# Gated linear attention on one core: the steps in a new order and on other engines, and second inputs of GpSimd's additions two elements further

## The chip, the cores and the metric

The kernel runs on one core of a Trainium2 chip. The metric is the device time of one execution in microseconds (us). Five engines work side by side and meet through semaphores: TensorE (PE in the profile, its weight loads PEld), VectorE (DVE), ScalarE (ACT), GpSimd (POOL) and SyncE (SP), which issues all transfers here.

## The reference

Linear attention over 8 batches of 8 heads, followed by a gated projection with a causal convolution of five taps as the gate:

```python
q_s = exp(q - max(q, axis=-1)); q_s = q_s / (sum(q_s, axis=-1) + 1e-09)
k_s = exp(k - max(k, axis=2));  k_s = k_s / (sum(k_s, axis=2) + 1e-09)
kv = einsum('bhsd,bhse->bhde', k_s, v)
x = einsum('bhsd,bhde->bhse', q_s, kv)          # then (B, S, H * D) = (8, 576, 512)
gate_pre = sum over k of conv_w[k] * x shifted down by 4 - k rows
gate = 1 / (1 + exp(-gate_pre))
out = (gate * (x @ w_val)) @ w_out
```

All inputs are float32 (the weights arrive as 64-bit words, whose value the kernel rebuilds).

## The kernel before

One string, ORDER, names 975 steps. The kernel records them one by one, each on the engine that its last letter names (v VectorE, p GpSimd, a ScalarE), so each engine works through its own part of that string in order and waits where an operand isn't there. No loop and no scheduler decides anything.

First, eight slabs of weight words (steps load_words, part, field, scaled, signed, joined) become two float32 values each, a rounded high part and a rest (w_high, w_low). Beside that, for each batch b of eight: the softmax over q (q_max, q_sub, q_exp, q_sum; in batches 0 to 2 also q_mul and transposes by TensorE, in batches 3 to 7 a second copy of q with channels on partitions, from which the row values ql that q_spread has fetched are subtracted: qc_sub, qc_exp), the softmax over k (k_peak, k_row, k_spread fetch the maxima kmax; k_sub, k_exp), and then

- kv b and kv_norm: the product of k and v, one 64 by 64 block per head;
- attend b 0 and attend b 1: TensorE makes x, channels on partitions, 576 tokens, two blocks p of 128 channels each;
- for each block p: x_high and x_low split x in two parts; first b p and four steps tap b p j sum the convolution into the tile gate. A tap on VectorE is one instruction that reads x from PSUM and gate from SBUF. A tap that is written "a" is two: ScalarE makes the product far from x, then GpSimd adds far to gate, both in SBUF. Step sigmoid follows.

Tokens are then cut into nine runs i of 512 (8 x 576 = 9 x 512). value i m is 12 matmuls of 128x512 (three products of high and low parts over four blocks); gated i m j multiplies by the gate into the tile g; g_high and g_low split g; project i t is again 12 matmuls, and store i t scales by 0.5 and writes out. Run i needs x of batch i - 1 and, below 8, of batch i.

Line numbers in the profile: 283 and 288 k_sub, 367 q_sub, 380 q_mul, 432 qc_sub, 237 and 236 signed, 229 field, 515 a tap on VectorE, 518 and 519 its two instructions elsewhere, 501 x_low, 542 gated, 183 and 181 copies (x_high, g_high), 550 g_low, 535 value, 559 project, 479 attend, 450 kv.

Of the kernel before, what the change touches and what calls it, by code (L numbers as in the profile page):

```python
# [48 lines left out]
    k_raise 1 2, load_words 5, signed 1, kv_norm 0 0 a, kv_norm 0 1 a, q_sum 1 a, q_turn 0 0, q_turned 0 0 a, w_low 2
    p, q_mul 1 2 p, load_kc 1 1, k_top 1 1, q_turn 0 1, q_turn 0 3, q_mul 1 0 v, q_turned 0 1 a, attend 0 0,  # L50
    load_words 4, field 4, q_mul 1 3 p, w_high 3 a, q_turned 0 3 a, w_low 3 v, first 0 0 a, tap 0 0 1 v, q_mul 1 1 p,
    q_turn 1 1, first 0 1 a, tap 0 1 2 a, load_kc 1 0, k_top 1 0, load_km 2 1, scaled 4 a, signed 4, part 1 a, joined
# [579 lines left out]
```

## Time and profile before

| | us |
|---|---|
| median of 3 runs (lowest, highest) | 322.35 (321.4, 323.44) |
| the profiled execution | 324.02 |
| its span, first to last instruction | 322.2 |
| busy in the span: PE, DVE, POOL, ACT | 272.3, 271.6, 229.0, 201.8 |

The profile is one execution. Its span lacks 1.8 us of its own time, and that execution lies 1.7 us above the median of the runs. Busy time is not work: an instruction that has been started and waits for its operands' ports counts as busy, and a matmul's recorded length overlaps the next one's. How long a matmul holds the engine is read from a long chain of them, as length over count.

### The profile page before, as it was taken

The numbers are of one execution on the slowest core, as the hardware profiler recorded it, in microseconds if no ns is written. First come the engines' busy times: TensorE is split into PE (matmuls) and PEld (weight loads), VectorE is DVE, ScalarE is ACT, GpSimd is POOL, SyncE is SP. The second block draws the span as 40 slices with busy tenths as digits, with TensorE's granted clock in tenths as the row PEclk, the third lists the DMA queues.
The fourth block names the chain that finished last, engine by engine and source line by source line (L and its number), as shares of the span: only waits on it lengthen the run. The fifth ranks groups of instructions, "written<-read, shape, count | busy, mean of one in ns | idle before, by whom it ended". The sixth has DMA issues, their size and how long they took to land.

```text
span 322.2 us, 5134 instructions
## 1 busy us (share of the span) xinstructions
PE 272.3 (85%) x1854; PEld 206.8 (64%) x1854; DVE 271.6 (84%) x399; ACT 201.8 (63%) x318; POOL 229.0 (71%) x187
## 2 busy tenths in 40 slices
PE   0264526899988999989999899999899999999995
PEld 0154413677766578757877586777577867888883
DVE  3999999999999999998999998999967886672330
ACT  2694776888789559885968696488715546431011
POOL 2696879489997899989878788788734935165210
PEclk9998755999999999999999999999979999999999
DMA  7999167449887756984948769953746201000123
GB/s 237 386 389 399 35 240 316 163 179 379 303 294 241 221 121 215 355 262 103 269 168 215 190 235 291 257 170 157 228 174 167 73 2 65 33 35 1 65 79 117
DMA packets 21800, 63.05 MB, mean 196 GB/s; under 512 B 3472, under 2 KB 7696, under 8 KB 18448
## 3 DMA queue, kind: packets, MB, share of 16 engines
q1 hardware_dynamic: 21776, 62.74, 57.8%
q8 instruction: 14, 0.23, 0.3%
q14 instruction: 10, 0.08, 0.1%
HBM read 53.19 MB, written 9.54 MB: 195 GB/s over the span
## 4 chain that ended last, share of the span: by engine, by line
DVE 50%; PE 28%; DMA 6%; issue 6%; ACT 5%; POOL 3%; SPq 0%; DVEq 0%; ACTq 0%; POOLq 0%
PE out L559 17%; PE val L535 9%; DVE gate L515 8%; DVE qs L374 5%; DVE xx L501 4%; DVE qm L364 4%; DVE g L542 3%; DMA ql<-qrow 3%; DVE kpk L269 3%; DVE qT L432 3%; DVE k L283 2%; DVE e L237 2%; DVE e L229 2%; DVE e L236 2%; PE x L479 2%
## 5 line engine op out<-in xcount | busy, mean ns | idle before, releaser
L519 POOL TENSOR_TENSOR gate<-gate,far 128x573 f32<-128x573 f32 (+3 forms) x57 | 79.2, 1394 | 40.0 <-ACT far L518 38.7
L535 PE MATMUL val<-xx,w_val_hi 128*128 128x512 f32 x288 | 89.9, 393 | 0.9 <-DVE xx L501 0.9
L535 PEld LDWEIGHTS val<-xx,w_val_hi 128*128 128x128 f32 x288 | 54.1, 188 | 12.7 <-DVE xx L501 1.3
L535 PE MATMUL val<-xx,w_val_lo 128*128 128x512 f32 x144 | 58.2, 404 | 3.5 <-DVE g L542 1.2
L559 PE MATMUL out<-w_out_lo,gh 128*128 128x512 f32 x144 | 58.7, 407 | 2.3 <-DVE gh L183 1.8
L559 PE MATMUL out<-w_out_hi,gl 128*128 128x512 f32 x144 | 58.0, 403 | 2.6 <-DVE gl L550 2.4
L515 DVE SCALAR_TENSOR_TENSOR gate<-x,cw,gate 128x572 f32<-128x572 f32 (+3 forms) x71 | 56.5, 806 | 1.3 <-POOL gate L519 0.4
L559 PE MATMUL out<-w_out_hi,gh 128*128 128x512 f32 x144 | 57.4, 399 | 0.0
L518 ACT ACTIVATE far<-x,cw 128x573 f32<-128x573 f32 (+3 forms) x57 | 41.5, 747 | 22.7 <-DVE gate L515 11.1
L550 POOL TENSOR_TENSOR gl<-g,gh 128x512 fp32r<-128x512 f32 x24 | 31.9, 1336 | 13.8 <-PE out L559 6.4
L542 DVE SCALAR_TENSOR_TENSOR g<-gate,val 128x320 f32<-128x320 f32 (+7 forms) x64 | 26.8, 446 | 12.4 <-POOL gl L550 5.3
L367 POOL TENSOR_TENSOR q<-q,qm 128x576 f32<-128x576 f32 x24 | 31.9, 1347 | 6.2 <-DVE qm L364 3.1
L535 PEld LDWEIGHTS val<-xx,w_val_lo 128*128 128x128 f32 x144 | 27.0, 188 | 14.0 <-issue 3.9
L187 ACT ACTIVATE o<-out 128x512 f32<-128x512 f32 x27 | 16.0, 601 | 31.8 <-PE out L559 16.2
L559 PEld LDWEIGHTS out<-w_out_lo,gh 128*128 128x128 f32 x144 | 27.4, 190 | 11.8 <-DVE gh L183 3.5
L559 PEld LDWEIGHTS out<-w_out_hi,gl 128*128 128x128 f32 x144 | 27.4, 190 | 11.3 <-DVE gl L550 4.2
L559 PEld LDWEIGHTS out<-w_out_hi,gh 128*128 128x128 f32 x144 | 27.5, 191 | 6.2
L501 DVE TENSOR_TENSOR xx<-x,xx 128x512 fp32r<-128x512 f32 (+7 forms) x64 | 27.4, 446 | 2.7 <-ACT xx L181 1.8
L524 ACT ACTIVATE gate<-gate 128x576 f32<-128x576 f32 x32 | 21.9, 691 | 10.0 <-DVE gate L515 5.4
L181 ACT CAST xx<-x 128x320 fp32r<-128x320 f32 (+7 forms) x54 | 20.6, 410 | 11.3 <-PE x L479 10.1
L479 PE MATMUL x<-qT,kvd 64*64 64x288 f32 x256 | 22.4, 442 | 5.3 <-DVE xx L501 2.7
L507 ACT ACTIVATE gate<-x,cw 128x576 f32<-128x576 f32 x27 | 19.8, 750 | 10.0 <-PE x L479 5.1
(71 smaller groups left out, 460.3 us busy)
## 6 DMA issues: line engine op xcount, KB each, us to landing
v<-in_v SPq DMA_DIRECT2D x8, 1170.0 KB, 7.6
...
km<-in_k_strided SPq DMA_DIRECT2D x12, 576.0 KB, 6.1
...
ql<-qrow SPq DMA_DIRECT2D x10, 576.0 KB, 7.3
...
```

The costliest lines, as they stand in the source:

```text
L181: nc.scalar.copy(out=out, in_=in_)
L367: engine(e).tensor_sub(groups(b, h), groups(b, h), wide(T["qm", b], h))
L479: nc.tensor.matmul(x[half][o, t], kvd[b % 2][r, n], T["qT", b][r, n, t], start=True, stop=True)
L501: nc.vector.tensor_sub(xx(i, p)[:, n], T["x", b, p][:, t], xx(i, p)[:, o].bitcast(F32))
L515: nc.vector.scalar_tensor_tensor(out=a, in0=x, scalar=w, in1=a, op0=ALU.mult, op1=ALU.add)
L518: nc.scalar.activation(part, x, AF.Copy, scale=w)
L519: nc.gpsimd.tensor_add(a, a, part)
L524: nc.scalar.activation(T["gate", b, p], T["gate", b, p], AF.Tanh, scale=0.5)
L535: nc.tensor.matmul(ps, a[:, kb, ms], z, start=(kb == 0 and j == 0), stop=(kb == NB - 1 and j == 2))
L542: nc.vector.scalar_tensor_tensor(out=T["g", i, m][:, o], in0=T["gate", b, m][:, t], scalar=1.0, in1=T["val", i, m][:, o], op0=ALU.add, op1 ...
L550: engine(e).tensor_sub(T["gl", i, m], T["g", i, m], T["gh", i, m].bitcast(F32))
L559: nc.tensor.matmul(ps, a, z[:, kb], start=(kb == 0 and j == 0), stop=(kb == NB - 1 and j == 2))
```

## The change

No step is added or taken away: the 975 steps of before stand in a new order, and some are given to another engine. Counted by step:

| step | before | after |
|---|---|---|
| tap | 71 v, 57 a | 88 v, 40 a |
| k_sub | 11 v, 19 p | 4 v, 26 p |
| qc_sub | 10 v, 10 p | 3 v, 17 p |
| q_sub | 8 v, 24 p | 4 v, 28 p |
| g_high | 12 v, 14 p, 10 a | 8 v, 12 p, 16 a |
| g_low | 12 v, 24 p | 14 v, 22 p |
| kv_norm | 9 v, 7 a | 5 v, 11 a |
| q_level | 3 v, 2 p | 0 v, 5 p |
| w_low | 1 v, 7 p | 0 v, 8 p |
| w_high | 7 a, 1 p | 6 a, 2 p |
| x_high | 10 v, 54 a | 12 v, 52 a |
| store | 9 v, 27 a | 10 v, 26 a |

The rest of the diff lets one of the two SBUF operands of GpSimd's additions and subtractions start two elements (8 bytes) further into its tile, which gets two more elements:

```diff
 ORDER = [step.strip() for step in """
-    load_words 8, field 8, part 8 v, load_q 0 r, load_words 0, part 0 a, scaled 8 v, signed 8, joined 8 p, q_max 0 r,
...
+    8 a, g_high 8 1 v, g_low 8 2 v, value 8 3, gated 8 3 1, g_high 8 3 v, g_low 8 3 v, g_low 8 1 p, project 8 0, store
...
-        f = T["f", i] = block("f", f"f{i}", 2, I32, C)[:, :lo.shape[1]]
+        f = T["f", i] = block("f", f"f{i}", 2, I32, C + 2)[:, 2:lo.shape[1] + 2]
...
-        t = T["kmax", b] = small.tile([P, C], F32, tag="kmax", name=f"kmax_{b}", bufs=1)
+        t = T["kmax", b] = small.tile([P, C + 2], F32, tag="kmax", name=f"kmax_{b}", bufs=1)[:, 2:]
...
-            T["ql", b] = big(f"ql{b}").rearrange("p (n s) -> p n s", n=NB)
+            T["ql", b] = big(f"ql{b}", S * NB + 2)[:, 2:].rearrange("p (n s) -> p n s", n=NB)
...
-            part = block("far", f"far_{b}_{p}_{j}", 2, F32, S)[:, :S - n]
+            o = 0 if n in (2, 3) else 2
+            part = block("far", f"far_{b}_{p}_{j}", 2, F32, S + 2)[:, o:o + S - n]
...
-            T["g", i, m] = block("g", f"g_{i}_{m}", 2)
+            T["g", i, m] = block("g", f"g_{i}_{m}", 2, F32, C + 2)[:, 2:]
```

A tap adds far, read from its first element, to gate, read from element n = 4 - j. Before, the two inputs of the addition therefore start n elements apart; n is 1 in the instructions of 575 elements, 2 in those of 574, 3 in those of 573 and 4 in those of 572. The subtractions k_sub, qc_sub, g_low and w_low and the addition joined read both inputs from the first element of their tiles, save that q_sub and q_mul read a [128, 9] tile spread over 64 columns, which the change leaves as it is. Afterwards the distance, counted modulo four elements, is two in k_sub, qc_sub, g_low, w_low, joined and the taps of 572 and 574, and three in those of 573 and 575.

VectorE in the rows that end with the last x_low that the first value product needs (words, e and f are weights, kpk the maxima of k, gate and xx are made from x), before:

```order
L367 TENSOR_TENSOR q_353<-q_353,qm_363 128x576
L515 SCALAR_TENSOR_TENSOR gate_1_330<-x_1_304,cw,gate_1_330 128x572
L501 TENSOR_TENSOR xx_1_361<-x_1_304,xx_1_361 128x64
L269 TENSOR_REDUCE kpk_424<-km_1_337 128x2
L236 TENSOR_SCALAR e_418<-e_418 128x512
L237 SCALAR_TENSOR_TENSOR e_418<-words_388,e_418 128x512
L236 TENSOR_SCALAR e_399<-e_399 128x512
L237 SCALAR_TENSOR_TENSOR e_399<-words_263,e_399 128x512
L269 TENSOR_REDUCE kpk_424<-km_0_386 128x2
L515 SCALAR_TENSOR_TENSOR gate_3_470<-x_3_450,cw,gate_3_470 128x572
L501 TENSOR_TENSOR xx_3_468<-x_3_450,xx_3_468 128x512
L501 TENSOR_TENSOR xx_2_475<-x_2_449,xx_2_475 128x512
```

and after:

```order
L229 TENSOR_SCALAR e_386<-words_336 128x512
L501 TENSOR_TENSOR xx_1_383<-x_1_302,xx_1_383 128x512
L515 SCALAR_TENSOR_TENSOR gate_0_317<-x_0_301,cw,gate_0_317 128x574
L515 SCALAR_TENSOR_TENSOR gate_1_324<-x_1_302,cw,gate_1_324 128x572
L229 TENSOR_SCALAR e_419<-words_417 128x512
L236 TENSOR_SCALAR e_386<-e_386 128x512
L237 SCALAR_TENSOR_TENSOR e_386<-words_336,e_386 128x512
L269 TENSOR_REDUCE kpk_441<-km_0_395 128x2
L501 TENSOR_TENSOR xx_2_467<-x_2_457,xx_2_467 128x512
L269 TENSOR_REDUCE kpk_441<-km_1_449 128x2
L515 SCALAR_TENSOR_TENSOR gate_3_470<-x_3_458,cw,gate_3_470 128x573
L501 TENSOR_TENSOR xx_3_477<-x_3_458,xx_3_477 128x512
```

Before, two pairs for the weights' signs (lines 236 and 237) and a subtraction from q stand here; after, one pair and one more tap, and the other pair has moved behind the x_low.

VectorE around the subtractions of batch 5's kmax from k (line 283), among taps of batch 4, before:

```order
L283 TENSOR_TENSOR k_1594<-k_1594,kmax_1588 128x512 x2
L501 TENSOR_TENSOR xx_1_1736<-x_1_1690,xx_1_1736 128x320
L515 SCALAR_TENSOR_TENSOR gate_1_1732<-x_1_1690,cw,gate_1_1732 128x575
L283 TENSOR_TENSOR k_1594<-k_1594,kmax_1588 128x512
L515 SCALAR_TENSOR_TENSOR gate_1_1732<-x_1_1690,cw,gate_1_1732 128x573
L515 SCALAR_TENSOR_TENSOR gate_1_1732<-x_1_1690,cw,gate_1_1732 128x572
L501 TENSOR_TENSOR xx_1_1425<-x_1_1690,xx_1_1425 128x256
L515 SCALAR_TENSOR_TENSOR gate_1_1732<-x_1_1690,cw,gate_1_1732 128x574
L501 TENSOR_TENSOR xx_0_1440<-x_0_1689,xx_0_1440 128x256
L501 TENSOR_TENSOR xx_0_1755<-x_0_1689,xx_0_1755 128x320
L364 TENSOR_REDUCE qm_1809<-q_1516 128x36
L283 TENSOR_TENSOR k_1594<-k_1594,kmax_1588 128x512
```

and after:

```order
L283 TENSOR_TENSOR k_1599<-k_1599,kmax_1619 128x512
L501 TENSOR_TENSOR xx_2_1507<-x_2_1778,xx_2_1507 128x256
L515 SCALAR_TENSOR_TENSOR gate_3_1794<-x_3_1779,cw,gate_3_1794 128x572
L515 SCALAR_TENSOR_TENSOR gate_2_1789<-x_2_1778,cw,gate_2_1789 128x573
L501 TENSOR_TENSOR xx_3_1478<-x_3_1779,xx_3_1478 128x256
L515 SCALAR_TENSOR_TENSOR gate_2_1789<-x_2_1778,cw,gate_2_1789 128x572
L501 TENSOR_TENSOR xx_3_1836<-x_3_1779,xx_3_1836 128x320
L543 SCALAR_TENSOR_TENSOR g_0_1841<-gate_0_1326,val_0_1820 128x256
L543 SCALAR_TENSOR_TENSOR g_0_1841<-gate_0_1682,val_0_1820 128x256
L515 SCALAR_TENSOR_TENSOR gate_3_1794<-x_3_1779,cw,gate_3_1794 128x574
L515 SCALAR_TENSOR_TENSOR gate_2_1789<-x_2_1778,cw,gate_2_1789 128x574
L515 SCALAR_TENSOR_TENSOR gate_3_1794<-x_3_1779,cw,gate_3_1794 128x575
```

Four of the five subtractions of this batch stand here before, one after; taps stand in their place.

GpSimd around the same subtractions, before:

```order
L519 TENSOR_TENSOR gate_0_1710<-gate_0_1710,far_0_3_1742 128x575
L367 TENSOR_TENSOR q_1314<-q_1314,qm_1475 128x576
L519 TENSOR_TENSOR gate_0_1710<-gate_0_1710,far_0_0_1748 128x572
L519 TENSOR_TENSOR gate_0_1710<-gate_0_1710,far_0_2_1788 128x574
L288 TENSOR_TENSOR k_1594<-k_1594,kmax_1588 64x256 x2
L367 TENSOR_TENSOR q_1516<-q_1516,qm_1809 128x576
L519 TENSOR_TENSOR gate_2_1812<-gate_2_1812,far_2_2_1827 128x574
L367 TENSOR_TENSOR q_1516<-q_1516,qm_1809 128x576 x2
L183 CAST gh_0_1888<-g_0_1862 128x512
L550 TENSOR_TENSOR gl_0_1890<-g_0_1862,gh_0_1888 128x512
L432 TENSOR_TENSOR qT_1734<-qT_1734,ql_1740 128x576 x3
```

and after:

```order
L520 TENSOR_TENSOR gate_0_1682<-gate_0_1682,far_0_1_1716 128x573
L520 TENSOR_TENSOR gate_0_1682<-gate_0_1682,far_0_2_1719 128x574
L283 TENSOR_TENSOR k_1599<-k_1599,kmax_1619 128x512
L288 TENSOR_TENSOR k_1599<-k_1599,kmax_1619 64x256 x2
L283 TENSOR_TENSOR k_1599<-k_1599,kmax_1619 128x512 x2
L432 TENSOR_TENSOR qT_996<-qT_996,ql_1709 128x576 x2
L183 CAST gh_0_1858<-g_0_1841 128x512
L551 TENSOR_TENSOR gl_0_1879<-g_0_1841,gh_0_1858 128x512
L183 CAST gh_1_1924<-g_1_1875 128x512
L418 TENSOR_TENSOR qs_1714<-qs_1714,qm_1439 128x36
L551 TENSOR_TENSOR gl_1_1954<-g_1_1875,gh_1_1924 128x512
```

The three other subtractions of 128x512 now stand here beside the one of 64x256, and four additions of a far tile have become two.

## Rows read from the trace of the kernel before

**Rows 1.** Chain that ended last, near the end: start us, us, what.

```profile
272.80 1.13 PE x L479 x16
273.93 19.44 PE val L535 x84
```

**Rows 2.** Busy time of all engines in two stretches: us, busy us (xinstructions) by engine, clock, DMA.

```profile
58.30:273.80 215.50, 204.00 (x1482) 153.23 (x1482) 200.35 (x304) 154.81 (x239) 172.54 (x135) 0.99 0.63 204
273.80:318.60 44.80, 44.76 (x196) 35.93 (x192) 18.60 (x31) 9.34 (x16) 14.69 (x14) 1.00 0.14 53
```

**Rows 3.** The first stretch again, for lines 535 and 450 alone.

```profile
58.30:273.80 215.50, 82.60 (x336) 61.78 (x336) 0.99 0.63 204
...
58.30:273.80 215.50, 19.51 (x560) 17.11 (x560) 0.99 0.63 204
```

**Rows 4.** PE waits from 61.3 to 273.8 us: us, times, longest.

```profile
PE out L559 <- DVE gl L550: 2.4, 4, 1.1
PE out L559 <- DVE gh L183: 1.8, 2, 1.1
PE x L479 <- DVE gate L515: 1.2, 1, 1.2
```

**Rows 5.** PE in order of time, where the first value product waits.

```profile
61.39 0.50 PE L535 MATMUL val<-xx,w_val_hi 128*128 128x512 f32 x1 [0.91 <-DVE xx L501]
```

**Rows 6.** DVE lines by source: duration ns min/median/max.

```profile
L237 DVE SCALAR_TENSOR_TENSOR e<-words,e x8: 691/1522/1648, 9.2 to 70.2; 128x512 int32<-128x512 int32 x8
...
L283 DVE TENSOR_TENSOR k<-k,kmax x10: 676/890/1691, 95.4 to 245.5; 128x512 f32<-128x512 f32 x10
...
L367 DVE TENSOR_TENSOR q<-q,qm x8: 744/1404/1776, 8.0 to 186.6; 128x576 f32<-128x576 f32 x8
...
L432 DVE TENSOR_TENSOR qT<-qT,ql x10: 747/1384/1725, 124.8 to 266.6; 128x576 f32<-128x576 f32 x10
...
L515 DVE SCALAR_TENSOR_TENSOR gate<-x,cw,gate x71: 795/805/818, 38.6 to 283.1; 128x572 f32<-128x572 f32 x20, 128x574 f32<-128x574 f32 x19, 128x573 f32<-128x573 f32 x16, 128x575 f32<-128x575 f32 x16
```

**Rows 7.** DVE, then POOL, in order of time from 172 us: start us, us.

```profile
172.08 3.25 DVE L283 TENSOR_TENSOR k<-k,kmax 128x512 f32<-128x512 f32 x2
...
173.18 1.60 POOL L367 TENSOR_TENSOR q<-q,qm 128x576 f32<-128x576 f32 x1
```

**Rows 8.** DVE groups by shape: xcount, busy us, mean ns, idle before.

```profile
L432 DVE TENSOR_TENSOR qT<-qT,ql 128x576 f32<-128x576 f32 x10 | 13.2, 1318 | 0.0
L550 DVE TENSOR_TENSOR gl<-g,gh 128x512 fp32r<-128x512 f32 x12 | 13.1, 1090 | 5.1 <-PE out L559 2.9 <-ACT gh L181 1.4 <-POOL gh L183 0.7
...
L367 DVE TENSOR_TENSOR q<-q,qm 128x576 f32<-128x576 f32 x8 | 10.6, 1325 | 0.0
L283 DVE TENSOR_TENSOR k<-k,kmax 128x512 f32<-128x512 f32 x10 | 10.5, 1054 | 0.0
L237 DVE SCALAR_TENSOR_TENSOR e<-words,e 128x512 int32<-128x512 int32 x8 | 9.9, 1238 | 0.3
L183 DVE CAST gh<-g 128x512 fp32r<-128x512 f32 x12 | 9.7, 807 | 0.3
```

**Rows 9.** POOL groups by shape.

```profile
L519 POOL TENSOR_TENSOR gate<-gate,far 128x575 f32<-128x575 f32 x16 | 25.1, 1570 | 12.2 <-ACT far L518 11.9
L519 POOL TENSOR_TENSOR gate<-gate,far 128x573 f32<-128x573 f32 x16 | 20.4, 1279 | 9.0 <-ACT far L518 8.7
L283 POOL TENSOR_TENSOR k<-k,kmax 128x512 f32<-128x512 f32 x14 | 20.0, 1441 | 1.2 <-DMA kmax<-krow 1.1
L519 POOL TENSOR_TENSOR gate<-gate,far 128x572 f32<-128x572 f32 x12 | 17.4, 1451 | 12.5 <-ACT far L518 12.2
L519 POOL TENSOR_TENSOR gate<-gate,far 128x574 f32<-128x574 f32 x13 | 16.4, 1265 | 6.3 <-ACT far L518 5.8
L432 POOL TENSOR_TENSOR qT<-qT,ql 128x576 f32<-128x576 f32 x10 | 15.8, 1596 | 0.0
```

**Rows 10.** DMA issues by line: count, KB each, median us to landing.

```profile
ql<-qrow SPq DMA_DIRECT2D x10, 576.0 KB, 7.3
```

More of the change, by code (lines that the diff above doesn't have):

```diff
@@ L49 @@
[L49 to L52, printed above, removed]
-    1 p, tap 0 1 1 a, x_high 0 0 1 a, k_raise 1 1, part 4 a, load_q 2 a, joined 4 p, x_high 0 1 0 a, k_raise 1 0,
@@ L89 @@
-    store 1 2 a, q_log 4, gated 2 1 0, qc_sub 3 0 v, k_sub 4 1 p, gated 2 1 1, x_low 2 2 1, tap 2 2 0 v, sigmoid 2 2,
-    tap 2 3 0 v, project 1 1, k_sub 4 2 p, kv 3, g_high 2 1 p, g_low 2 1 p, qc_exp 3 0, q_level 4 p, kv_norm 3 0 a,
-    tap 2 3 2 v, kv_norm 3 1 a, load_q 6 a, load_km 6 1, sigmoid 2 3, load_v 4, q_row 4, value 2 3, attend 3 0, k_sub
-    4 4 p, x_high 3 0 0 a, g_high 2 0 v, first 3 1 a, q_max 5 a, q_sub 5 2 p, g_low 2 0 v, gated 2 3 1, x_high 3 1 0
-    a, k_sub 4 3 p, gated 2 3 0, g_high 2 3 p, g_low 2 3 p, first 3 0 a, k_sub 4 0 v, tap 3 1 2 a, q_sub 5 0 p, value
@@ L134 @@
-    4 p, first 6 3 v, tap 6 3 1 v, tap 6 3 0 v, tap 6 2 2 a, q_spread 7 1, k_sub 7 1 p, value 6 0, x_high 6 2 1 a,
-    x_low 6 2 1, k_exp 7, gated 6 0 0, gated 6 0 1, g_high 6 0 p, project 5 2, value 6 2, store 5 2 v, tap 6 2 1 v,
-    g_low 6 1 p, tap 6 2 3 v, kv 7, store 5 0 a, x_low 6 3 1, g_low 6 0 p, gated 6 2 1, tap 6 3 3 a, sigmoid 6 2,
-    gated 6 2 0, value 6 3, qc_sub 7 0 v, kv_norm 7 0 a, qc_sub 7 1 v, qc_exp 7 0, tap 6 3 2 v, gated 6 3 1, sigmoid 6
-    3, gated 6 3 0, qc_sub 7 3 p, attend 7 0, g_high 6 3 a, g_low 6 3 v, g_high 6 2 p, first 7 1 a, tap 7 1 0 v,
@@ new lines @@
+    1 2 1, k_peak 4 1, k_row 4, q_sub 4 2 p, gated 1 1 0, q_exp 3 a, kv_norm 2 0 a, q_sum 3 a, q_log 3, q_sub 4 3 v,
+    g_high 1 1 a, tap 1 2 1 v, load_km 5 0, tap 1 3 2 v, q_level 3 p, g_low 1 1 p, sigmoid 1 3, k_sub 3 4 p, value 1
+    3, gated 1 3 1, gated 1 0 1, load_qc 5, k_sub 3 1 p, attend 2 0, gated 1 3 0, x_high 2 1 0 v, sigmoid 1 2, gated 1
+    0 0, g_high 1 3 a, x_low 2 1 0, value 1 2, first 2 0 a, g_low 1 3 p, g_high 1 0 a, g_low 1 0 p, tap 2 0 1 v, gated
+    1 2 1, q_row 3, gated 1 2 0, g_high 1 2 v, x_high 2 0 1 a, first 2 1 a, g_low 1 2 v, load_qc 3, x_high 2 1 1 a,
@@ new lines @@
+    4 2 3 v, sigmoid 4 2, qc_sub 5 1 p, qc_sub 5 0 p, qc_exp 5 0, g_high 4 0 p, load_v 6, value 4 1, gated 4 1 0,
+    load_k 6, g_low 4 0 p, gated 4 1 1, kv 5, g_high 4 1 p, q_level 6 p, x_low 4 2 1, kv_norm 5 1 a, kv_norm 5 0 a,
+    value 4 2, tap 4 3 1 v, k_peak 7 0, g_low 4 1 p, store 3 3 a, sigmoid 4 3, q_sub 7 0 p, gated 4 2 0, gated 4 2 1,
+    qc_sub 5 2 p, q_row 6, g_high 4 2 a, attend 5 0, k_spread 6, x_high 5 1 0 a, value 4 3, g_low 4 2 p, qc_sub 5 3 v,
+    x_low 5 1 0, first 5 0 a, x_high 5 0 0 a, tap 5 0 0 v, x_high 5 1 1 a, x_low 5 1 1, gated 4 3 1, gated 4 3 0, tap
@@ new lines @@
+    6 0, x_low 5 2 1, k_sub 6 2 p, k_sub 6 3 v, k_sub 6 1 p, sigmoid 5 2, gated 5 2 0, k_sub 6 0 p, load_km 7 1, store
+    4 0 a, store 4 1 v, tap 5 3 3 v, gated 5 2 1, project 4 3, g_high 5 0 p, g_high 5 2 p, sigmoid 5 1, q_sum 7 a,
+    x_low 5 3 1, g_low 5 0 p, tap 5 3 0 v, k_exp 6, kv 6, qc_sub 6 0 p, q_log 7, load_qc 7, qc_sub 6 1 p, kv_norm 6 0
+    v, qc_exp 6 0, store 4 3 a, sigmoid 5 3, value 5 1, kv_norm 6 1 v, q_level 7 p, q_row 7, k_peak 7 1, k_row 7,
+    attend 6 0, x_high 6 0 0 a, gated 5 1 1, g_low 5 2 v, gated 5 1 0, x_high 6 0 1 a, first 6 1 a, tap 6 1 0 v,
```

191 lines of the change are left out of this document (96 added, 95 removed).

## The prediction

> **What bounds the kernel now.** I read the chain of waits from its end first. From 273.93 us to the end TensorE runs value and output products back to back: 84 matmuls in 19.44 us, 0.231 us each, right behind the last attend, 1.13 us long [rows 1]. In that tail TensorE is busy 44.76 of 44.8 us and VectorE 18.6 [rows 2]. Sixteen of the 72 product groups lie behind the last attend before the change, and sixteen after it, so the tail costs the same 45 us. What can change is when the last attend comes.
>
> Before it the picture turns over. From 58.3 to 273.8 us, the stretch from the first value product, VectorE is busy 200.35 of 215.5 us and GpSimd 172.5 [rows 2]. TensorE shows 204, but that is recorded length, not work. The matmuls of line 535 in this stretch are 336, 28 groups of 12 [rows 3], and by the order of steps as many of line 559 lie there: 672 at 0.231 make 155.5 us. 14 attends at 1.13 make 15.8, the seven kv 19.5 [rows 3], and 26 small transposes of q, taken at half a product matmul, 3. That is 194 us of work in 215.5: about 21 us of slack. The larger waits of TensorE there are for VectorE's g_low and its copies of g [rows 4], and the first value product itself waits until 61.39 for VectorE's x_low [rows 5]. So the kernel is VectorE's up to the last attend, TensorE's behind it, and VectorE can give back at most the slack and an earlier start.
>
> **Why VectorE is slow.** The rows that carry the argument are minima beside means. A subtraction of ql lasts 0.747 us at best, 1.384 in the middle, 1.725 at worst; k_sub spreads from 0.676 to 1.691, q_sub from 0.744 to 1.776, the sign step of line 237 from 0.691 to 1.648. All of these read two SBUF tiles. A tap, one input from PSUM, stays between 0.795 and 0.818 over 71 instructions [rows 6]. The timeline shows what is waited for: from 172.08 us two k_sub take 3.25 us on VectorE while GpSimd works without a pause, and its own q_sub there takes 1.60 [rows 7]; I read that as the two taking turns. Busy time less count times minimum gives the time lost in four lines: 5.7 (432), 4.6 (367), 3.7 (283), 4.4 (237), 18.4 us in 36 instructions, 0.5 us each [rows 6, 8].
>
> **The change on VectorE.** At means of before, which contain that loss: seven k_sub fewer at 1.054, 7.4; seven qc_sub at 1.318, 9.2; four q_sub at 1.325, 5.3; four g_high at 0.807, 3.2: 25.1 us out [rows 8]. In come 17 taps at 0.805 [rows 6], 13.7; two g_low at 1.090 [rows 8], 2.2; a store and two x_high, from PSUM as a tap is, at most 2.4: 18.3 us. Net -6.8. One w_low, three q_level and four short kv_norm leave too; no row here prices them. They can't cost by leaving; I take 0.5 each, -4, between 0 and -8. What remains of the colliding kinds (8 sign steps, 14 g_low, 8 g_high, 10 subtractions) is 40, losing 20 us at 0.5 each. If the new order puts them where GpSimd stands still, this goes; if it puts them worse, it can grow (a bound above: 1.0 each, the largest loss in rows 6, +20). I take -4, since the one thing that I can count is that GpSimd is somewhat less busy. VectorE: about -15, between +13 and -35.
>
> **The change on GpSimd.** At the means of its rows, 17 additions leave, about 1.4 each, -23.7; seven k_sub at 1.441 and seven qc_sub at 1.596 come, +21.3 [rows 9]; four q_sub, taken as k_sub, +5.8; w_low, w_high and three q_level less two g_low and two copies, near +3. Net +6. Then the two elements. Additions of 574 and 573 elements, inputs two and three apart, take 1.265 and 1.279 us; those of 575 and 572, one and four apart, 1.570 and 1.451; subtractions that start together take 1.441 for 512 and 1.596 for 576 elements [rows 9]. Length can't do this (575 against 574), distance can, and the change gives every such pair distance two or three. At 1.265 / 574 = 2.20 ns per element, 512 cost 1.13 and 576 1.27: 21 k_sub save 0.31 each, 17 qc_sub 0.33, 14 taps of 575 0.30, ten of 572 0.18, 38 of g_low, w_low and joined, if like k_sub, 0.31, together 30 us; since their mean may hold more waiting than the others' I take 24, between 0 (the distance was a coincidence) and 30. GpSimd: about -18 of 229. It is not the bound, so this counts in what waits for it and what collides with it, inside the -4 above.
>
> Against this stands the Trainium skill's GPSIMD Engine Reference, section Elementwise, side-by-side cycle accounting: two-input work costs about 2.6 cycles per element because both reads share one port. By that one price the shift would save GpSimd nothing, and I would add some 2 us to the forecast; rows 9 hold 2.20 and 2.73 ns per element side by side for one operation, which one price can't give.
>
> ScalarE loses 17 products of taps and gains six g_high; I cost that at nothing, hidden by its idle time: neither of the larger waits of TensorE names it [rows 4].
>
> **The start.** Up to the x_low that the first value needs, VectorE has nine taps instead of four (+4.0 at 0.805), two q_mul instead of one (+1.3 as a q_sub), no w_low (-1.1 as a g_low) and one pair of sign steps less (-2.5 as two of line 237) [rows 6, 8]: +1.7. Some 24 colliding instructions there lose 0.5 each, 12 us; GpSimd has seven additions fewer ahead of that place, near 10 us of its 60, and faster ones. I take a third of the 12 off: -4. Start: -2.3, between +1.7 and -10.
>
> **The sum.** Start -2.3. Of VectorE's other -12 TensorE can't use all: its 21 us of slack include the changes from one kind of product to another and stalls at hand-overs that stay. I take 8, between 0 and 14. Together -10.3 on a span of 322.2, so 311.9, and 313.7 for an execution like the profiled one, whose 324.02 lies 1.67 above the median of 322.35. Against that median: 312.0 us.
>
> **Rivals.** (1) The collisions nearly vanish. Start -6 to -8, TensorE's slack down by 13: -19 to -21, 301.5 to 303.5; with half of it 307. For it: the 40 remaining are few enough to be put into GpSimd's pauses, and half of what is taken from VectorE is exactly the kind that collides. Against it: GpSimd stays over 70% busy.
>
> (2) Nothing comes of it. 17 subtractions that VectorE gives away run on GpSimd in a row, so the remaining 40 meet a GpSimd with fewer pauses and lose 0.7 instead of 0.5 us each; that 8 us eats the -6.8, and the start's +1.7 its gain: 320 to 324. It decides from 0.65 us per instruction on. The Trainium skill's Perfetto Trace Analysis, section Optimizing Scalar/DVE Operations, says that moving work between VectorE and GpSimd might not help since they share an SBUF port. Against it speaks that taps, which replace the subtractions, show no loss in any of 71 instructions [rows 6].
>
> (3) Slower: the first value starts later. VectorE's +1.7 there is certain if the losses stay; the transfers ahead of the first kv are one weight slab more (0.5 MB), which I price at 1.5 us, a fifth of what a transfer of that size needs to land [rows 10], since several are under way at once; the -4 fails to come. Each us goes straight to the end: start +3.5, TensorE's slack unchanged, 326. It decides where the losses in the start don't fall by at least 2 us.
>
> (4) The rows of ql and kmax now land 8 bytes past their old place. A transfer of ql takes 7.3 us [rows 10]; no transfer of before lands at such a place, so nothing in the trace prices it. Were it twice as long in five batches, with half of it uncovered, +18 less the 10: 330.
>
> **How the numbers follow.** A measurement of this kernel tells about 1%, 3.2 us, from no change. Forecast (308 to 317): 0.62. Rival 1, fuller gains (300 to 308): 0.19. Rival 2: 0.10. Rival 3: 0.06. Rival 4: 0.03. Faster by over 1% (below 319.1): 0.81; within 1%: 0.11; slower: 0.08. The range leaves out the lower quarter of rival 1 and most of 2 to 4: 303.5 to 320.
>
> **What would show it.** Right: additions of 572 and 575 elements near 1.2 to 1.3 us and k_sub on GpSimd near 1.1; VectorE busy 250 to 260 us; the first value product's last wait before 60 us; the last attend near 264 us and a tail of 45 behind it. Wrong: a VectorE still near 270 us busy, whose remaining subtractions have medians at the worst of rows 6 (then rival 2); a first value behind 62 us (rival 3); subtractions of ql that wait for a DMA (rival 4). A tail longer than 46 us would mean that the order starves TensorE behind the last attend, which I hold for excluded by a VectorE that is idle for more than half of it [rows 2].

## The result and the profile after

| us | before | after |
|---|---|---|
| median (lowest, highest) | 322.89 (321.40, 323.55), 4 runs | 304.14 (303.24, 304.45), 4 runs |
| the profiled execution, its span | 324.02, 322.2 | 304.37, 302.6 |
| busy PE, DVE, POOL, ACT | 272.3, 271.6, 229.0, 201.8 | 267.6, 237.6, 194.4, 193.5 |

The ratio is 0.9421, 95% interval 0.9379 to 0.9463: 18.7 us faster where 10.3 were forecast. The time lies in the range (303.5 to 320), 0.6 us from its fast end, close to where rival 1 put it (301.5 to 303.5).

The page's chain that ended last, first before, by engine, then after, by engine and by line:

```profile
DVE 50%; PE 28%; DMA 6%; issue 6%; ACT 5%; POOL 3%; SPq 0%; DVEq 0%; ACTq 0%; POOLq 0%
```

```profile
PE 81%; DVE 10%; ACT 4%; DMA 2%; issue 1%; SPq 1%; DVEq 0%; ACTq 0%
PE val L536 32%; PE out L560 32%; PE kv L450 8%; PE x L479 7%; DMA q<-in_q 2%; DVE gate L515 1%; DVE gl L551 1%; PE qps L386 1%; DVE ktop L304 1%; DVE qm L364 1%; DVE qs L374 1%; DVE g L543 1%; ACT kc L201 1%; ACT gate L507 1%; DVE e L229 1%
```

The chain went through VectorE for half of the span; now it goes through TensorE for four fifths. (From line 518 of before on, every line now stands one further down.) The chain near the end, after: start us, us, what.

```profile
253.48 1.13 PE x L479 x16
254.61 1.60 PE val L536 x6
```

Busy time of all engines between the first value product and the last attend, and behind it; the columns are those of [rows 2] (after the us: busy us and instructions of PE, PEld, DVE, ACT and POOL, then granted clock, DMA share, GB/s):

```profile
50.60:254.60 204.00, 199.15 (x1482) 151.41 (x1480) 177.13 (x291) 149.99 (x235) 155.62 (x148) 1.00 0.68 214
254.60:299.00 44.40, 44.36 (x194) 35.95 (x192) 18.04 (x33) 10.74 (x19) 9.77 (x9) 1.00 0.12 48
```

So the 19.6 us of span come from three places. The first value product starts at 50.66 instead of 58.37: 7.7. From there to the end of the last attend (273.93 before [rows 1], 254.61 now) 204.0 us pass instead of 215.6: 11.6. The tail gives the 0.3 that is left. In the middle stretch the same 1482 matmuls now keep TensorE busy for 199.15 of 204.0 us, while VectorE, which had been busy for 200.35 of 215.5 [rows 2], has 27 us to spare. Of the 11.6 us, 6.6 are waits of TensorE (11.4 before, 4.8 after, all gaps added up). The rest is recorded busy time of the same matmuls, and part of that is its clock: before, behind waits of 0.74 and 1.08 us for g_high and g_low, the granted clock fell to 0.50 (the lower of its two levels, 1.2 and 2.4 GHz), and the matmuls came 0.43 us apart instead of 0.23; after has no such stretch.

```profile
234.90:238.30 3.40, 3.40 (x10) 2.62 (x9) 3.26 (x8) 0.00 (x0) 2.23 (x2) 0.50 0.37 157
```

What TensorE still waits for in after: us, times, longest; and its row at the first value product (kvd is what kv_norm makes).

```profile
PE out L560 <- DVE gh L183: 1.6, 1, 1.6
PE out L560 <- DVE gl L551: 1.5, 2, 0.9
PE x L479 <- ACT kvd L470: 0.9, 1, 0.9
PE val L536 <- DVE xx L501: 0.8, 1, 0.8
```

```profile
54.26 0.50 PE L536 MATMUL val<-xx,w_val_hi 128*128 128x512 f32 x1 [0.79 <-DVE xx L501]
```

That is the wait of [rows 5], 7.1 us earlier. The VectorE lines of [rows 6], after, with min/median/max in ns:

```profile
L237 DVE SCALAR_TENSOR_TENSOR e<-words,e x8: 691/692/693, 8.6 to 57.7; 128x512 int32<-128x512 int32 x8
...
L283 DVE TENSOR_TENSOR k<-k,kmax x3: 682/909/1451, 169.8 to 232.2; 128x512 f32<-128x512 f32 x3
...
L367 DVE TENSOR_TENSOR q<-q,qm x4: 746/750/751, 7.4 to 148.4; 128x576 f32<-128x576 f32 x4
...
L432 DVE TENSOR_TENSOR qT<-qT,ql x3: 747/750/1034, 183.8 to 243.1; 128x576 f32<-128x576 f32 x3
...
L515 DVE SCALAR_TENSOR_TENSOR gate<-x,cw,gate x88: 792/806/817, 38.1 to 260.9; 128x574 f32<-128x574 f32 x24, 128x573 f32<-128x573 f32 x24, 128x572 f32<-128x572 f32 x22, 128x575 f32<-128x575 f32 x18
...
L551 DVE TENSOR_TENSOR gl<-g,gh x14: 672/693/1576, 100.9 to 289.3; 128x512 fp32r<-128x512 f32 x14
```

The minima are those of before, and the medians have come down to them, save that of k_sub, three of which are left (909, and 890 before). All eight sign steps last 691 to 693 ns, where the median was 1522. I take for each instruction its duration less the shortest of its shape, over all VectorE lines that read SBUF alone (the subtractions, sign steps, copies to g_high, g_low and the like): before 41.6 us are lost in 84 instructions, after 6.0 in 60 (which run's shortest is taken moves the larger of these sums by up to 2 us). The difference is about what VectorE's busy time fell (34.0). This sum is called the lost time below. The new order keeps the two apart: before, 69 of the 84 overlap an instruction of GpSimd by more than 50 ns, after 23 of the 60, while the taps lie beside one for 59 of their 71 us and lose nothing.

GpSimd's groups by shape, to be held against [rows 9]:

```profile
L283 POOL TENSOR_TENSOR k<-k,kmax 128x512 f32<-128x512 f32 x21 | 23.1, 1116 | 0.2
L432 POOL TENSOR_TENSOR qT<-qT,ql 128x576 f32<-128x576 f32 x17 | 21.2, 1259 | 0.0
L520 POOL TENSOR_TENSOR gate<-gate,far 128x575 f32<-128x575 f32 x14 | 17.9, 1282 | 7.3 <-ACT far L519 5.9 <-issue 1.2
L520 POOL TENSOR_TENSOR gate<-gate,far 128x572 f32<-128x572 f32 x10 | 12.0, 1199 | 10.3 <-ACT far L519 10.1
```

k_sub fell from 1.441 to 1.116, qc_sub from 1.596 to 1.259, the additions of 575 and 572 elements from 1.570 and 1.451 to 1.282 and 1.199. How much of that is the shift and how much are fewer collisions, the first three experiments tell. The transfers that land two elements further are no slower (7.3 us before [rows 10]):

```profile
ql<-qrow SPq DMA_DIRECT2D x10, 576.0 KB, 6.0
```

### The profile page after: what moved, and what is told of

Same layout as the page of the kernel before. It is cut to its first block, busy times and chain, and to the rows that moved or that the text cites. A ratio compares the mean times of both kernels' runs of the same rounds, so it can differ in the third digit from the quotient of the medians.

```text
span 302.6 us, 5110 instructions
## 1 busy us (share of the span) xinstructions
PE 267.6 (88%) x1854; PEld 205.9 (68%) x1854; DVE 237.6 (79%) x391; ACT 193.5 (64%) x311; POOL 194.4 (64%) x189
## 4 chain that ended last, share of the span: by engine, by line
PE 81%; DVE 10%; ACT 4%; DMA 2%; issue 1%; SPq 1%; DVEq 0%; ACTq 0%
PE val L536 32%; PE out L560 32%; PE kv L450 8%; PE x L479 7%; DMA q<-in_q 2%; DVE gate L515 1%; DVE gl L551 1%; PE qps L386 1%; DVE ktop L304 1%; DVE qm L364 1%; DVE qs L374 1%; DVE g L543 1%; ACT kc L201 1%; ACT gate L507 1%; DVE e L229 1%
## 5 line engine op out<-in xcount | busy, mean ns | idle before, releaser
L515 DVE SCALAR_TENSOR_TENSOR gate<-x,cw,gate 128x574 f32<-128x574 f32 (+3 forms) x88 | 70.0, 807 | 4.9 <-ACT gate L507 2.8
L520 POOL TENSOR_TENSOR gate<-gate,far 128x575 f32<-128x575 f32 (+3 forms) x40 | 50.1, 1255 | 32.1 <-ACT far L519 30.0
L560 PE MATMUL out<-w_out_lo,gh 128*128 128x512 f32 x144 | 57.3, 398 | 1.6 <-DVE gh L183 1.6
L519 ACT ACTIVATE far<-x,cw 128x575 f32<-128x575 f32 (+3 forms) x40 | 29.1, 757 | 12.9 <-DVE xx L501 5.1
L543 DVE SCALAR_TENSOR_TENSOR g<-gate,val 128x64 f32<-128x64 f32 (+7 forms) x64 | 26.8, 449 | 12.8 <-PE val L536 11.9
L560 PEld LDWEIGHTS out<-w_out_lo,gh 128*128 128x128 f32 x144 | 27.0, 188 | 10.3 <-issue 2.6
L551 POOL TENSOR_TENSOR gl<-g,gh 128x512 fp32r<-128x512 f32 x22 | 24.1, 1100 | 15.2 <-ACT gh L181 7.6
L501 DVE TENSOR_TENSOR xx<-x,xx 128x256 fp32r<-128x256 f32 (+7 forms) x64 | 27.6, 448 | 7.0 <-ACT xx L181 6.5
L181 ACT CAST xx<-x 128x512 fp32r<-128x512 f32 (+7 forms) x52 | 20.7, 413 | 14.2 <-PE x L479 8.7
L450 PEld LDWEIGHTS kv<-v,k 128*64 128x64 f32 (+1 forms) x640 | 21.1, 145 | 4.6 <-issue 1.1
L450 PE MATMUL kv<-v,k 128*64 128x65 f32 (+1 forms) x640 | 24.0, 238 | 0.0
```

Source lines behind the costliest of these rows:

```text
L450: nc.tensor.matmul(to, kk[r, o:o + D], vv[r, c * H + n], start=(c == 0), stop=(c == 4))
L501: nc.vector.tensor_sub(xx(i, p)[:, n], T["x", b, p][:, t], xx(i, p)[:, o].bitcast(F32))
L515: nc.vector.scalar_tensor_tensor(out=a, in0=x, scalar=w, in1=a, op0=ALU.mult, op1=ALU.add)
L519: nc.scalar.activation(part, x, AF.Copy, scale=w)
L520: nc.gpsimd.tensor_add(a, a, part)
L543: nc.vector.scalar_tensor_tensor(out=T["g", i, m][:, o], in0=T["gate", b, m][:, t], scalar=1.0, in1=T["val", i, m][:, o], op0=ALU.add, op1 ...
```

## The experiments

**1 and 2. The two halves of the change.** The first keeps the order and engines of before and takes only the tiles; the second the other way round:

```diff
-        f = T["f", i] = block("f", f"f{i}", 2, I32, C)[:, :lo.shape[1]]
+        f = T["f", i] = block("f", f"f{i}", 2, I32, C + 2)[:, 2:lo.shape[1] + 2]
```

and so for kmax, ql, far and g (experiment 2 has the ORDER of after and the minus lines).

> The order and engines of before with the five shifted tiles alone. Theory A (VectorE's lost time in collisions is the cause; GpSimd is not the bound, so its shorter additions count only through those collisions): GpSimd's additions of 572 and 575 elements fall to about 1.2 us where nothing holds them and its busy time falls by some 20 us, but the time falls by 1 to 4 us only, to 319 to 322, with VectorE still busy about 265 us. Theory B (the shift carries the gain): 304 to 312 us. Theory C (the distance was a coincidence): additions as before, 322 to 324 us.

319.27 us, ratio 0.9889 (0.984 to 0.9939). GpSimd's busy time falls from 229.0 to 207.6, VectorE's lost time only from 41.6 to 36.6. GpSimd by shape:

```profile
L520 POOL TENSOR_TENSOR gate<-gate,far 128x575 f32<-128x575 f32 x16 | 20.3, 1268 | 16.5 <-ACT far L519 16.2
L283 POOL TENSOR_TENSOR k<-k,kmax 128x512 f32<-128x512 f32 x14 | 17.8, 1283 | 1.8 <-DMA kmax<-krow 1.6
L432 POOL TENSOR_TENSOR qT<-qT,ql 128x576 f32<-128x576 f32 x10 | 12.9, 1308 | 0.0
```

21 us less work on an engine that isn't the bound are worth 3.2 us, by the medians (322.47 beside it): theory A.

> The order and engines of after with no tile shifted. Theory A: most of the gain is here, 305 to 310 us, with the sign steps of line 237 still near 0.69 us and VectorE busy 240 to 250 us; GpSimd's busy time 215 to 220 us. Theory B (the shift carries the gain): above 314 us. A third theory (order tuned so tightly to the shorter additions that without them it runs worse than before): above 323 us.

310.38 us (305.95 to 311.94 over 6 runs), ratio 0.9629 (0.9566 to 0.9693); lost time 8.2, GpSimd 216.6. That is theory A, 0.4 us above its interval. So the order and the engines carry two thirds of the gain, and the shift is worth 6 us on top of them, more than alone. The profiled execution was the fastest of the six; experiment 8 takes up the spread. GpSimd's subtractions there, still from distance zero, show the two halves apart: k_sub went from 1.441 to 1.313 with the order alone and to 1.116 with the shift on top, qc_sub from 1.596 to 1.492 and 1.259.

```profile
L283 POOL TENSOR_TENSOR k<-k,kmax 128x512 f32<-128x512 f32 x21 | 27.2, 1313 | 0.2
L432 POOL TENSOR_TENSOR qT<-qT,ql 128x576 f32<-128x576 f32 x17 | 25.2, 1492 | 0.0
```

**3. The prices by themselves.** A kernel that computes nothing of the reference: it times instructions alone and pairs of them side by side, on tiles in SBUF (x in PSUM).

```diff
+        for _ in range(8):
+            nc.gpsimd.tensor_add(c[:, 0:N], c[:, 0:N], d[:, 2:N + 2])
+            nc.vector.tensor_sub(a[:, :576], a[:, :576], e[:, :576])
```

> This kernel computes nothing of the reference: it times single instructions. Theory A: GpSimd alone adds 568 elements in about 1.2 us where its two inputs start 2 or 3 elements apart (modulo 4, whichever is moved) and in about 1.4 us at 0 or 1; VectorE alone takes 0.75 us for a subtraction of two SBUF tiles of 576, 0.69 for a tap with x in PSUM, 0.43 for a copy of 512 in SBUF; beside GpSimd's additions the subtraction and the copy take 1.2 to 1.9 us and the tap stays at 0.69. Rival (collisions are no more than the two engines' reading of the same tiles, or SBUF traffic at large): the tap is slowed beside GpSimd as much as the subtraction, or neither is, since the two engines here work on different tiles.

By shape, with the mean ns behind the comma. Additions of 568 elements on GpSimd alone, the first input starting 0 (L55) and 2 (L59) elements further into its tile than the second; a subtraction alone on VectorE (L76), and beside additions 2 apart (L88, L87); a tap beside the same additions (L93, L91):

```profile
L55 POOL TENSOR_TENSOR c<-c,d 128x568 f32<-128x568 f32 x4 | 5.5, 1378 | 0.2
L59 POOL TENSOR_TENSOR c<-c,d 128x568 f32<-128x568 f32 x4 | 4.8, 1188 | 0.3
L76 DVE TENSOR_TENSOR a<-a,e 128x576 f32<-128x576 f32 x8 | 6.1, 757 | 0.2
L88 DVE TENSOR_TENSOR a<-a,e 128x576 f32<-128x576 f32 x8 | 12.1, 1518 | 0.2
L87 POOL TENSOR_TENSOR c<-c,d 128x568 f32<-128x568 f32 x8 | 12.4, 1544 | 0.5
L93 DVE SCALAR_TENSOR_TENSOR a<-x,w,a 128x512 f32<-128x512 f32 x16 | 12.0, 750 | 0.5
L91 POOL TENSOR_TENSOR c<-c,d 128x568 f32<-128x568 f32 x8 | 9.5, 1188 | 0.6
```

Distances 0, 1 and 4 take 1.376 to 1.378 us, distances 2, 3 and 6 take 1.188; moving the second input instead by 1, 2 or 3, which is a distance of -1, -2 or -3, gives 1.189, 1.189, 1.380. So what counts is the start of the first input less that of the second, modulo four elements, and starting both at element 1 instead of 0 changes nothing (1.380). The sum is written over the first input here as in the kernel, so the output's place isn't told apart from that input's. A subtraction that takes 0.757 alone takes 1.518 beside GpSimd, and GpSimd's addition 1.544 instead of 1.188: both lose. A tap, which reads x from PSUM, and the addition beside it lose nothing. That this is the input from PSUM and not the kind of instruction, the kernel before shows: the sign step of line 237 has the operation of a tap on SBUF tiles and spreads from 0.691 to 1.648 [rows 6], and x_low, a TENSOR_TENSOR as the subtraction is but with x in PSUM, keeps 0.674 to 0.683:

```profile
L501 DVE TENSOR_TENSOR xx<-x,xx 128x512 fp32r<-128x512 f32 x8 | 5.3, 679 | 0.0
```

Both mechanisms of the prediction are hereby shown.

**4 and 5. The earlier start and the rest, apart.** Experiment 4 has the steps of after up to the first value product and those of before behind it; experiment 5 the reverse. Both have the shifted tiles, so experiment 1 (319.27) is what they start from.

What experiment 4 changes, in words: ORDER holds the steps of after through "value 0 0", then those of before that are left, in before's order and on before's engines. (A longer ORDER puts every line two further down in the profiles of experiments 4 to 7 and 11.)

> After, up to its first value product; from there the remaining steps in the order and on the engines of before, tiles shifted. In the profiles the first value product starts about 8 us earlier in after, and TensorE loses about 11 us less from there to the last attend. If these two parts add up (theory A), this kernel keeps the 8 and part of the shift's gain: 311 to 315 us, the first value product near 51 us. If the early start is worth nothing without the rest, because VectorE is still the bound behind it (rival): 318 to 322 us, TensorE's waits behind the first value longer by what the start gained.

318.56 us, ratio 0.9867 (0.9817 to 0.9916). The first value product starts at 50.83 instead of 58.25, and the last attend ends at 268.69 instead of 269.49. Windows from the one to the other:

```profile
50.80:268.70 217.90, 205.05 (x1482) 153.70 (x1480) 199.21 (x308) 154.44 (x238) 155.38 (x136) 0.98 0.64 199
```

The rival's time: the 7.4 us of an earlier start are given back. VectorE has 199.21 us to do here, as it had before (200.35 [rows 2]). The giving back is over by 71 us, close behind the place where the two orders are joined. TensorE's wait there (us, times, longest) and the window around its end:

```profile
PE val L538 <- DVE g L545: 4.5, 2, 4.1
64.20:71.00 6.80, 5.89 (x16) 4.10 (x20) 5.89 (x8) 4.52 (x9) 5.50 (x5) 0.50 0.79 290
```

TensorE waits once for 4.14 us, until 65.1, for VectorE's g, and its granted clock is 0.50 from 64.2 to 71.0; from there to the end its attends come 0.4 to 0.8 us ahead of experiment 1's. What the joint costs and what a busy VectorE costs aren't told apart.

> The steps of before up to the first value product, then the order and engines of after, with the shifted tiles: the counterpart of the run that had the start of after alone. Theory A (VectorE's relief behind the first value is what lets TensorE run on, and the earlier start then adds to it whole): first value product near 58, last attend near 262, waits of TensorE between them about 5 to 6 us, 311 to 313 us. Rival (the new start is what keeps the engines apart later, so that the rest is worth little without it): waits of 9 us or more, last attend near 267, 316 us or more.

317.27 us, ratio 0.9856 (0.98 to 0.9912): the theory's 311 to 313 did not come; the time is the rival's. The rival's reason isn't borne out, however:

```profile
58.50:265.80 207.30, 199.81 (x1483) 151.69 (x1483) 176.43 (x288) 149.72 (x235) 153.09 (x147) 1.00 0.68 213
```

VectorE has the relief here (176.43 against 177.13 in after, lost time about 6 in this stretch). The stretch takes 207.3 us, where it took 211.2 with the shift alone and 204.0 in after, and TensorE waits for 7.5 us of it (4.8 in after). 2.5 of the 3.3 us beyond after are lost by 75 us, again close behind the joint, where TensorE waits 1.91 us for a copy by ScalarE (us, times, longest):

```profile
PE val L538 <- ACT k L183: 2.9, 2, 1.9
```

From there to 220 us its attends keep within 0.4 us of a fixed distance behind after's. So the relief does let TensorE run on as in after, and the theory failed at the joint, 0.9 us further on, and by 1.3 us that the median lies above the profiled execution. From experiment 1 the two parts are worth 0.7 and 2.0 us, together 15.1. Part of what is missing is the price of the joints; how much, in experiment 4 above all, isn't told apart. That the rest is one engine's limit, which hides the other's relief, is my reading.

**6 and 7. Sequence and engines, apart.** Experiment 6 has the sequence of after, each step on before's engine; 7 the sequence of before, each step on after's engine; both with the shift.

In words: every step keeps its place, and its last letter is the other kernel's.

> The sequence of steps of after, but each step on the engine that before gave it, with the shifted tiles. Theory A (the choice of engines keeps two-input work off VectorE, the sequence matters less): VectorE loses 20 us or more to GpSimd again, busy near 260, 314 to 319 us. Rival B (the sequence puts VectorE's two-input work where GpSimd stands still, whatever the engines): loss below 12 us, 305 to 309 us.

> The sequence of steps of before, but each step on the engine that after gives it, with the shifted tiles. Theory A (the choice of engines does it): VectorE loses under 15 us to GpSimd, busy 240 to 248, 308 to 313 us. Rival B (the sequence does it): loss of 25 us or more, 314 to 319 us. A third way is that subtractions on GpSimd come late in this sequence, so that TensorE waits for them: waits of TensorE above 12 us though VectorE is not busy.

377.95 us, ratio 1.1695 (1.1632 to 1.1758), and 351.72 us, ratio 1.0909 (1.086 to 1.0958). Both theories miss: neither half is worth anything with the wrong other half. It isn't work: VectorE is busy for 258.2 and 249.0 us, GpSimd for 203.0 and 198.7, less than before the change. It is waiting, and lost time of 26.6 and 16.9 us lies between before and after. TensorE waits for 41.3 and 28.4 us from the first value to the last attend. What GpSimd waited for most, in 6 (38.7 us before, 30.0 after):

```profile
POOL gate L522 <- ACT far L521: 86.7, 23, 14.3
```

I read it so: where a tap is given to ScalarE and GpSimd in a place made for VectorE, its first half comes when ScalarE is elsewhere in its queue, GpSimd stands until it does, and the gate behind it too. These two kernels therefore don't tell which half avoids the collisions; experiment 11 does so with a smaller step.

**8 to 10. The spread, and one wait.** Experiment 8 repeats experiment 2.

> The order and engines of after without the shift, once more, for the spread that it showed between executions (305.95 to 311.94) while its profile showed a fast one. If the spread is a difference of GpSimd's additions against VectorE's timing, a profile of a long execution has more lost time on VectorE than 8.2 us and TensorE waiting in other places; if it is TensorE's clock, the granted clock is lower with the same waits. Time 306 to 312 us again.

310.56 us (309.61 to 312.0), ratio 0.9632 (0.959 to 0.9673), lost time 8.6: the first idea is out. Against the short execution of experiment 2 (span 304.2) the profiled one (310.2) is 3.75 us later at the first value product and 2.3 longer from there to the last attend. TensorE in order of time where it waits longest, and the windows around it:

```profile
163.61 0.59 PE L559 MATMUL out<-w_out_lo,gh 128*128 128x512 f32 x1 [1.82 <-DVE gh L183]
...
165.43 0.80 PE L559 MATMUL out<-w_out_hi,gl 128*128 128x512 f32 x1 [0.80 <-DVE gl L550]
```

```profile
158.00:163.60 5.60, 3.79 (x17) 2.75 (x15) 5.50 (x8) 4.72 (x6) 4.79 (x4) 1.00 0.95 357
163.60:170.00 6.40, 5.59 (x13) 3.90 (x14) 6.40 (x4) 4.22 (x7) 6.32 (x5) 0.52 0.91 189
```

Behind the wait the granted clock falls from 1.00 to about half, its lower level, and the next 28 product matmuls take 9.18 us instead of 6.64. After has the same wait at the same step:

```profile
159.36 0.50 PE L560 MATMUL out<-w_out_lo,gh 128*128 128x512 f32 x1 [1.62 <-DVE gh L183]
...
160.97 0.50 PE L560 MATMUL out<-w_out_hi,gl 128*128 128x512 f32 x1 [0.88 <-DVE gl L551]
```

and keeps its clock; experiment 2's execution waited 1.83 and 1.08 there and kept it too. A wait of this length can cost twice and doesn't always. (The Trainium skill's TensorE: Matmul & The Clock Gate, Part 1: The HAM clock gate, says that the number of slow matmuls at a kernel's start differs between runs of one kernel. The traces agree for the start, as the open point below shows, and here a stretch in the middle differs too.) VectorE in after just ahead of it, and GpSimd beside it:

```profile
155.49 1.66 DVE L515 SCALAR_TENSOR_TENSOR gate<-x,cw,gate 128x573 f32<-128x573 f32 x2
157.07 0.74 DVE L543 SCALAR_TENSOR_TENSOR g<-gate,val 128x320 f32<-128x320 f32 x2
157.84 1.46 DVE L183 CAST gh<-g 128x512 fp32r<-128x512 f32 x1
159.34 1.58 DVE L551 TENSOR_TENSOR gl<-g,gh 128x512 fp32r<-128x512 f32 x1
157.83 5.43 POOL L520 TENSOR_TENSOR gate<-gate,far 128x572 f32<-128x572 f32 x4 [1.19 <-ACT far L519]
```

Two taps stand ahead of the product g, and g_high and g_low (0.43 and 0.69 at best) then meet GpSimd's four additions, which begin at 157.83. So the second of the two taps is moved, in after (9) and in experiment 2's kernel (10):

```diff
-    load_km 6 1, x_low 4 0 0, first 4 1 a, q_exp 6 a, g_low 3 1 v, tap 4 1 1 v, tap 4 1 2 v, first 4 0 a, qc_sub 4 3
-    p, tap 4 0 0 a, tap 4 0 3 a, gated 3 2 0, gated 3 2 1, g_high 3 2 v, g_low 3 2 v, tap 4 1 3 a, x_high 4 0 1 a, tap
+    load_km 6 1, x_low 4 0 0, first 4 1 a, q_exp 6 a, g_low 3 1 v, tap 4 1 1 v,  first 4 0 a, qc_sub 4 3
+    p, tap 4 0 0 a, tap 4 0 3 a, gated 3 2 0, gated 3 2 1, g_high 3 2 v, g_low 3 2 v, tap 4 1 2 v, tap 4 1 3 a, x_high 4 0 1 a, tap
```

> The kernel after, with one step moved: of the two taps that VectorE runs at 155.49 us, the second comes behind the g_low that TensorE waits for at 159.36 and 160.97 (1.62 and 0.88 us). Theory (VectorE's place in line is what TensorE waits for, and GpSimd's additions, which start at 157.83, stretch the g_high and g_low that come late): the product g is made at 156.5, g_high and g_low no longer meet GpSimd's additions, both waits fall to under 0.4 each, and everything behind comes 2 us earlier: 301.5 to 302.5 us. Rival: the tap that comes later delays the next value product or GpSimd's addition behind it by as much, or the wait turns up one stage later: 304 us.

301.97 us (301.18 to 302.98, 5 runs), ratio 0.9367 (0.9337 to 0.9396), in the theory's interval and the fastest kernel here: 2.2 us under after, whose four runs all lie above these five. VectorE:

```profile
154.91 0.80 DVE L515 SCALAR_TENSOR_TENSOR gate<-x,cw,gate 128x573 f32<-128x573 f32 x1
...
156.60 0.43 DVE L183 CAST gh<-g 128x512 fp32r<-128x512 f32 x1
157.06 0.69 DVE L551 TENSOR_TENSOR gl<-g,gh 128x512 fp32r<-128x512 f32 x1
```

Both collisions are gone with the place, and both waits of TensorE at this step. Of the 2.5 us of span (302.6 to 300.1), 1.65 lie between the first value product and the last attend, where the wait for kvd grew from 0.9 to 1.4; 0.8 lie ahead of the first value product, where nothing was changed.

> The order and engines of after without the shift (310.5 us), with the same one step moved. There the waits at 163.61 and 165.43 us (1.82 and 0.80) stand before a stretch with a granted clock of 0.50, in which 28 product matmuls take 9.18 us, where after's take 6.64. Theory (such a wait costs twice, by itself and by the clock that falls behind it): 2.6 us of wait less 0.4 that stays, and 2.5 of slow clock go, 305 to 307 us, and the spread narrows. Rival (the clock falls for another reason, the wait alone is saved): 308 to 309 us.

306.75 us (305.64 to 307.67, 6 runs), ratio 0.9506 (0.9479 to 0.9533), in the theory's interval: 3.8 us under experiment 8, more than the 2.6 of the two waits, and the spread is 2.0 us instead of 2.4 and 6.0. The two profiles bear this out: their attends run within 0.1 us of each other up to 156 us, and from 190 us on experiment 10 is 4.3 ahead. Since the clock kept its level behind the same waits in experiment 2's profile, the price of the clock is shown for one execution and not for each.

**11. The subtractions back on VectorE.**

In words: k_sub, q_sub and qc_sub, in after 11 v and 71 p, go each to the engine that before gave it, 29 v and 53 p; all else is as in after.

> The kernel after, with k_sub, q_sub and qc_sub on the engines that before gave them (26 back on VectorE, 8 on GpSimd instead), the taps and the sequence as in after. Theory A (18 more two-input subtractions on VectorE cost it their time and the turns with GpSimd): VectorE's lost time rises from 6 to 12 us or more, its busy time to 258 or more, TensorE waits for it again by 10 us or more: 314 to 325 us. Rival (the places in the sequence are ones where GpSimd stands still, so that they cost VectorE 0.75 each and fill its idle time): lost time under 8, busy near 251, 305 to 310 us.

319.7 us (318.59 to 322.26, 7 runs), ratio 0.9924 (0.9892 to 0.9957): theory A, save that VectorE's busy time of 254.0 stays under the 258 named. VectorE's rows for qc_sub, k_sub and q_sub, min/median/max:

```profile
L434 DVE TENSOR_TENSOR qT<-qT,ql x10: 742/750/1758, 117.3 to 260.1; 128x576 f32<-128x576 f32 x10
L285 DVE TENSOR_TENSOR k<-k,kmax x10: 675/762/1690, 80.8 to 235.2; 128x512 f32<-128x512 f32 x10
L369 DVE TENSOR_TENSOR q<-q,qm x8: 746/750/1625, 7.6 to 201.6; 128x576 f32<-128x576 f32 x8
```

More than half now run near their minimum, so the sequence does keep the engines apart (lost time 12.1, against 36.6 in experiment 1). But 18 instructions more on VectorE, 16 us in all, fill what it had to spare, TensorE waits for 12.9 us instead of 4.8, and all that the order gave beyond experiment 1 is gone. The moved subtractions are a part that the gain can't do without.

## Why the prediction was right, and what it mis-sized

The mechanism was right at each link, and most sizes were not: VectorE was the bound up to the last attend, its SBUF-only work lost time to GpSimd while taps didn't (experiment 3), the shift shortens GpSimd's instructions (experiments 1 and 3), and TensorE becomes the bound behind the first value product. That the range held is in part luck: the time lies 0.6 us inside it, 7.9 us under the forecast of 312.0 and outside the 308 to 317 that had 0.62. Of the signs that were named, two failed with it (VectorE busy for 250 to 260 us, the last attend near 264: 237.6 and 254.61); the rest came. Most terms of the sum were too small, and one had the wrong sign.

- **Tail 45 us, unchanged.** Right: 44.4.
- **Collisions of the 40 that remain, -4.** The step that failed most. The sign steps, g_low, g_high and subtractions that stay lose 5.1 us instead of the 20 that I carried over, so the term is -15; lines 229 and 236, which I hadn't counted among the colliding ones, give another 7.6 (8.5 lost before, 0.9 after). I took a value near nothing since GpSimd was only somewhat less busy. Busy share was the wrong measure: GpSimd is still busy for 156 of 204 us in the middle stretch, but most of VectorE's pieces stand in its pauses, and where they don't (experiment 9's two) one step's place decides it. The swap itself is worth next to nothing: at minima 14.7 us of subtractions and copies go out, and 13.7 of taps and 1.4 of g_low come in.
- **VectorE -15, so 257 us busy.** Measured -34.0, 237.6: the same error, carried on.
- **GpSimd -18.** Measured -34.6. The shift's -24 holds (experiment 1: -21.4). The moves, put at +6, are -12.4 (experiment 2): GpSimd's instructions shed their half of the collisions too, which I charged to VectorE alone: its q_sub, which the shift leaves as it is, fell from a mean of 1.347 us to 1.173 in experiment 2.
- **The two elements inside the -4.** Right that they count little alone (3.2 us), wrong that they count little at all: on top of the order they are worth 6. Between experiment 8 and after, 0.9 lies at the start, 1.2 in the wait for kvd (2.09 and 0.86 us), and most of the rest in the stretches of lower clock behind that wait (0.66 from 68 to 73 us) and the one at 163.61.
- **Start -2.3.** Measured -7.7. The 24 colliding instructions ahead of the first value lose 0.8 us, not two thirds of 12; I had seen the 12 and taken a third. (GpSimd runs five additions fewer ahead of that place, not seven.)
- **TensorE's slack, -8.** Measured -11.6, inside the bounds. The 21 us that I counted were too many, since TensorE is still busy for 199 us here, where it hardly waits, and not for 194; of the 16.3 that this leaves, seven tenths came. The sum also had no term for TensorE's clock, which before fell behind the waits at 232 and 234 us; eight matmuls there, 0.19 us longer each, make 1.6 us. Experiments 4 and 5, which have start and slack apart, don't show the two adding up, and part of that is their joints.
- **Rival 1** forecast a start of -6 to -8, a slack of -13 and 301.5 to 303.5 us. It is what happened, but for 1.4 us of slack. Its 0.19 was too little by what came; no row of before shows where the new order puts the 40.
- **Rivals 2, 3, 4.** The loss per remaining instruction is about 0.1 us, not 0.7; the first value comes earlier; the transfers of ql land no later. Of the Trainium skill's two rules: that moving work between VectorE and GpSimd might not help (Perfetto Trace Analysis, Optimizing Scalar/DVE Operations) is borne out by experiment 3 for instructions that run side by side, and answered here by an order in which few do. The one price for two-input work (the Trainium skill's GPSIMD Engine Reference, Elementwise, side-by-side cycle accounting) is contradicted: 1.188 and 1.378 us for the same addition, by the distance of its inputs.

Open: why executions of experiments 2 and 8 differ by up to 3.75 us ahead of the first value product. 2.1 us of it stand there when the first kv begins. The other 1.6 lie in that block, which takes 2.78 us in the one and 4.41 in the other, and go with the clock: the trace's first record of it, a granted 1.00, starts at 23.5 us in experiment 2, ahead of the block (24.9), and at 30.8 in experiment 8, near its end (31.4). Ahead of these records there is none, though the window view prints 1.00 there; the matmuls of the block come 0.054 us apart ahead of the record in experiment 8 and 0.029 behind it in experiment 2. Why the clock rose later no run here takes apart.
